# The second layer of an expert block, one half of its rows after the other

## The chip, the core and the metric

The kernel runs on one core of a Trainium2 chip. The metric is the device time of one execution in microseconds (us). The kernel before took 558.54 us, the median of three runs (556.77 to 562.39). The engines are TensorE (PE in the rows; PEld is its weight load), VectorE (DVE), ScalarE (ACT), GpSimd (POOL) and SyncE (SP). Each takes its instructions in the order of its own queue.

## The reference, cut to what matters

A global filter, then a mixture of experts with one expert for each token:

```
X = rfft(x, axis=1);  Y = X * F;  y = irfft(Y)            # x: 8 x 2496 x 256
x = y.reshape(19968, 256)
logits = x @ w_gate + modality_bias[modality_id]          # 8 experts
e_idx = argmax(logits);  gate_w = softmax(logits)[e_idx]
for e in range(8):
    h = relu(x[e_idx == e] @ w1[e])                       # 256 -> 1024
    out[e_idx == e] = gate_w * (h @ w2[e])                # 1024 -> 256
```

## The kernel before, in words

The filter is done as a two-stage Fourier transform by matmuls, for eight groups of 2496 tokens. When a group is done, its tokens are routed, and GpSimd scatters their rows to bins in DRAM by expert (`scatter`, line 786; 20 indirect DMAs for a group). From then on blocks of 256 tokens of one expert are taken from the bins and sent through the two layers, while the next groups are still being transformed. 79 blocks are computed in this draw. The three kinds of work (transform, routing, blocks) lie beside each other until the last group is routed; then only blocks are left.

A block is 256 rows, as two halves of 128 rows (`NI` = 2). The first layer gives `hT`, 1024 hidden columns as eight tiles (`FT` = 8) of 128 partitions by 256 rows. `up(b, q)`, for q from 0 to 3, does two of these tiles: four matmuls (line 945) into a PSUM tile `hps`, and one Relu on ScalarE (line 950) into `hT`. `down(b, q)` is the second layer: in each step it takes the two hidden tiles that belong to q, and for each of them both halves of the rows: four matmuls (line 958) that add to `ops`, a PSUM tile of 128 x 2 x 256 float32, where the first index of the free part is the half. Both halves lie in one 2 KiB bank of PSUM. There are two buffers of `ops`.

`step()` sets the order in which the block's work is written: `up` of the current block, `down` of the block before it, with the same q. So between two steps of `down` there are four matmuls of `up`. At q = 1 the next block is prepared (`turn`): VectorE copies the expert's first weights to `w1` (line 913), later also the second weights to `w2` (line 920), and, in the first 44 blocks, the block's transposed rows to `xT` (line 932).

After the last step of `down`, VectorE multiplies each half of `ops` by the gates of its rows into `osb` (line 970, two instructions), and GpSimd scatters both halves to the output (line 972, two indirect DMAs). `osb` has three buffers; later, every other block takes a buffer of another pool of three, so that a buffer is used again six blocks on. A new tile of `osb` is taken when the gate is written, and its first write waits until both scatters from the old tile in that buffer have landed.

In the first part of the program the order on TensorE, ScalarE and VectorE is as written. In the part with the blocks a scheduler sets the order of instructions on each engine when the program is built, from its own estimates; it also places the waits. Two rules of the code bind it on GpSimd: a scatter to the bins is issued behind the last scatter to the output written before it (`behind("out", 1)`), and it waits for a matmul written shortly before (`paced`).

Of the kernel before, what the change touches and what calls it, by code (L numbers as in the profile page):

```python
# [12 lines left out]
F32 = mybir.dt.float32  # L13
# [5 lines left out]
IOA = bass.IndirectOffsetOnAxis  # L19
ET = mybir.EngineType  # L20

P = 128
# [7 lines left out]
def kernel(  # L30
# [12 lines left out]
    nc = tc.nc  # L43

    B, S, D = x.shape
    NF = S // 2 + 1
    N = B * S
# [5 lines left out]
    FT = F // P  # L53
# [18 lines left out]
    NI = BLK // P  # L72
# [48 lines left out]
    xp = ctx.enter_context(tc.tile_pool(name="fx", bufs=3))  # L121
# [18 lines left out]
    marks = {"ld": [], "up": [], "w1": [], "out": [], "pe": []}  # L140
# [40 lines left out]
    def row_int(expr_ops, base, name):  # L181

        t = fft_pool.tile([P, 1], I, name=name + "_int")
        nc.vector.tensor_copy(t, base)
        for op, v in expr_ops:
            nc.vector.tensor_single_scalar(t, t, v, op=op)
        f = fft_pool.tile([P, 1], F32, name=name)
        nc.vector.tensor_copy(f, t)
        return f
# [26 lines left out]
    NP = NTT // EV  # L216
# [141 lines left out]
    with tc.manual_schedule():  # L358
# [14 lines left out]
        for f_dram, g in ((filt_r, g1), (filt_i, g2)):  # L373
# [5 lines left out]
            out=Lexcl, in_=Lexcl, compare_op=ALU.is_ge, fill=1.0,  # L379
# [8 lines left out]
        half = row_int([(ALU.arith_shift_right, 1)], rows_i, "half")  # L388
# [87 lines left out]
        for s0 in range(0, NS, SPB):  # L476
            for src, dst in ((w2m, a1m), (w2x, a2m)):
                tp = pp.tile([P, EV * D], F32, tag="ps", name="tp")
                for i in range(SPB):
                    nc.tensor.matmul(tp[:KB, i * KB:(i + 1) * KB], lhsT=src[:, s0 + i, :], rhs=perm,  # L480
                                     start=True, stop=True)
# [21 lines left out]
    w2sb = wpool.tile([P, E, FT, D], BF16)  # L503
# [292 lines left out]
    def free_of(ins, group):  # L796
        tc.declare_no_dep(ins.ins, group=group, reason="disjoint rows")
# [136 lines left out]
            nc.vector.tensor_copy(b["meta"], b["xs"][:, :, DW:DW + 2])  # L934

    FQ = 2
    turn_about = [False]

    def up(b, q):
        third = "xs" not in b and len(marks["up"]) % 3 == 2  # L940
        hps = (op if third else hp).tile([P, FQ, NI * P], F32, tag="tr" if third else "hps", name="hps")
        for k in range(FQ):
            ft = q * FQ + k
            for dc in range(DC):
# [4 lines left out]
        marks["pe"].append(mm.ins)  # L949
        nc.scalar.activation(b["hT"][:, q * FQ:(q + 1) * FQ, :], hps, AF.Relu)  # L950

    def down(b, q):
        if q == 0:
            b["ops"] = op.tile([P, NI, D], F32, tag="ops", bufs=2, name="ops")
        for k in range(FQ):
            ft = q * FQ + k
            for i in range(NI):
                nc.tensor.matmul(b["ops"][:, i, :], lhsT=b["hT"][:, ft, i * P:(i + 1) * P],  # L958
                                 rhs=b["w2"][:, ft, :] if b["still"] else w2sb[:, ds(b["e"], 1), ft, :],
                                 start=(ft == 0 and i == 0), stop=(ft == FT - 1 and i == NI - 1))  # L960
        if (q + 1) * FQ == FT:

            turn_about[0] ^= n > begin[B - 1] + NP
            if turn_about[0]:
                osb = xp.tile([P, NI, D], F32, tag="x", name="osb")
            else:
                osb = ep.tile([P, NI, D], F32, tag="osb", bufs=3)
            gate = b["meta"][:, :, 1:2].bitcast(F32)
            for i in range(NI):
                nc.vector.tensor_scalar_mul(osb[:, i, :], b["ops"][:, i, :], gate[:, i, :])  # L970
            for i in range(NI):
                ins = nc.gpsimd.indirect_dma_start(  # L972
                    out=out[:, :], out_offset=IOA(ap=b["meta"][:, i, 0:1], axis=0),
                    in_=osb[:, i, :], in_offset=None, bounds_check=N - 1, oob_is_err=False)
                marks["out"].append(ins.ins)
                free_of(ins, "outs")
                tc.add_to_no_dep_group("outs", ins.ins)

    def pad_bins():

# [11 lines left out]
    class Experts:  # L992
# [36 lines left out]
        def step(self):  # L1029

            if self.q == 0:
                if self.cur is None:
                    self.cur = self.next()
                    self.begin(self.cur)
                self.nxt = None
            if self.cur is None and self.prev is None:
                return False
            if self.cur is not None:
                up(self.cur, self.q)
                if self.q == 1:  # L1040

                    self.nxt = self.next()
            if self.prev is not None:
                down(self.prev, self.q)
            if self.q == 1:
                self.begin(self.nxt)
            self.q += 1
            if self.q == FT // FQ:
                self.prev, self.cur, self.q = self.cur, self.nxt, 0
            return True  # L1050
# [51 lines left out]
    with tc.manual_schedule(engines={ET.PE, ET.Activation, ET.DVE}):  # L1102
# [141 lines left out]
        n = -2 * LONG  # L1244
# [20 lines left out]
    ep = ctx.enter_context(tc.tile_pool(name="expert", bufs=2, side="right", reuse_waits="tile"))  # L1265
# [9 lines left out]
    begin = [(g - TURNED - 2) * GAP for g in range(B)]  # L1275
# [5 lines left out]
    n = max(0, opening[0][1] + WAIT)  # L1281
# [3 lines left out]
    n = 0  # L1285
# [3 lines left out]
    while n <= end or to_bins or opening:  # L1289
# [3 lines left out]
        for g in range(TURNED + 1, B):  # L1293
            k = n - begin[g] - OFF2
# [6 lines left out]
        for g in range(TURNED, B):  # L1301
            k = n - begin[g] - OFF3
# [63 lines left out]
```

## Time and profile before

| | |
|---|---|
| median of three runs | 558.54 us (556.77 to 562.39) |
| the profiled execution | 557.56 us |
| its span, first to last instruction | 555.7 us |
| mean granted TensorE clock | 0.955 of full speed |
| busy share | PE 89%, DVE 68%, ACT 68%, POOL 70% |
| scatters on POOL | 158 to the output, 160 to the bins |

The span is 1.86 us shorter than the device time of the same execution. A row of a timeline gives the start, the duration, the engine, the line, the operation and how many instructions of that kind are merged in it (x4: four); in square brackets stands the idle time before it and who ended it. Matmuls are pipelined, and the duration of one includes its way through the array, so the ends of consecutive matmuls overlap the next starts.

### The profile page before, as it was taken

To read this page: it belongs to the slowest core of one execution; us is meant where nothing else is said; L and a number is where in the kernel's file an instruction comes from. 1 tells how busy PE (TensorE), PEld (TensorE's weight loads), DVE (VectorE), ACT (ScalarE), POOL (GpSimd) and SP (SyncE) were. 2 spreads that over 40 slices of the span, in tenths; PEclk is the share of its full clock that TensorE was granted. 3 is DMA by queue.
4 is the path that set the end of the run, shared out by engine and by line. 5 is a ranking of instruction groups with operands and counts; after the bars stand their busy time and mean duration, and the time that the engine had idled before them with its cause. 6 is when DMAs were issued, how large, how long until landed. Compare 5 with 4: busy or idle time off the path is not lost.

```text
span 555.7 us, 14830 instructions
## 1 busy us (share of the span) xinstructions
PE 493.6 (89%) x4933; PEld 451.8 (81%) x4933; DVE 377.7 (68%) x1139; ACT 376.0 (68%) x692; POOL 390.3 (70%) x427
## 2 busy tenths in 40 slices
PE   3699979687999898999999999998799989999992
PEld 2678868576988798898898988897689989999991
DVE  8866878643678678688879988863465555655541
ACT  4686866775787687788777765565466666666660
POOL 9633378585525776777777777777777777777773
PEclk9978889878999898999999999999899999999996
DMA  9989989779799899989868563253354445565521
GB/s 139 165 127 214 212 173 183 166 176 251 187 198 232 240 201 213 275 215 240 259 178 235 146 185 124 79 173 97 115 120 104 123 121 119 129 135 135 134 96 43
DMA packets 103112, 92.42 MB, mean 166 GB/s; under 512 B 40293, under 2 KB 86725, under 8 KB 102941
## 3 DMA queue, kind: packets, MB, share of 16 engines
q0 software_dynamic: 31936, 50.75, 40.3%
q1 hardware_dynamic: 47795, 29.16, 22.4%
q10 hardware_dynamic: 23302, 11.50, 7.8%
q8 instruction: 43, 0.70, 0.5%
q14 instruction: 36, 0.29, 0.2%
HBM read 60.10 MB, written 46.35 MB: 192 GB/s over the span
## 4 chain that ended last, share of the span: by engine, by line
PE 47%; DMA 25%; DVE 12%; issue 6%; ACT 4%; POOL 4%; DVEq 0%; SPq 0%; POOLq 0%; ACTq 0%
PE hps L945 13%; PE ops L958 13%; DMA out_dram<-osb,metas 11%; DMA bins_d<-yo,pos_i 4%; DMA b_d<-t 3%; DMA b_d<-z 3%; PE ps L545 3%; DMA t<-b_d 2%; PE pz L557 2%; PE lt L691 2%; PE pz L558 2%; PE ps L668 2%; DVE osb L970 2%; DVE xf L580 2%; PE ps L671 1%
## 5 line engine op out<-in xcount | busy, mean ns | idle before, releaser
L950 ACT ACTIVATE hT<-hps 128x512 f16<-128x512 f32 x316 | 187.9, 598 | 93.7 <-PE hps L945 89.2
L972 POOL DMA_INDIRECT out_dram<-osb,metas x158 | 167.7, 1062 | 55.3 <-issue 18.9
L786 POOL DMA_INDIRECT bins_d<-yo,pos_i x160 | 164.8, 1030 | 58.1 <-issue 28.8
L945 PE MATMUL hps<-xT,w 128*128 128x256 f16 x1264 | 200.0, 276 | 6.0 <-DVE xT L932 6.0
L945 PEld LDWEIGHTS <-w 128*128 128x128 f16 x1264 | 148.6, 145 | 10.6 <-DVE xT L932 6.8
L958 PEld LDWEIGHTS <-hT 128*128 128x128 f16 x1264 | 123.1, 98 | 17.9 <-issue 6.8
L958 PE MATMUL ops<-w2sb,hT 128*128 x704 | 113.0, 275 | 1.5 <-issue 1.4
L970 DVE TENSOR_SCALAR osb<-ops,metas 128x256 f32<-128x256 f32 x158 | 69.3, 476 | 46.9 <-DMA out_dram<-osb,metas 35.2
L958 PE MATMUL ops<-w,hT 128*128 128x256 f16 x560 | 83.3, 272 | 2.3 <-DVE osb L970 2.2
L913 DVE COPY w<-w1sb 128x2048 f16 x79 | 56.3, 712 | 41.2 <-PE hps L945 38.2
L572 ACT CAST xf<-ps 104x512 f16<-104x512 f32 x96 | 57.6, 600 | 9.7 <-PE ps L545 8.1
L579 DVE TENSOR_TENSOR p<-xf,g 104x512 f16<-104x512 f16 x96 | 40.2, 419 | 28.4 <-ACT xf L572 28.1
L594 ACT CAST z<-pz 104x512 f16<-104x512 f32 x72 | 42.7, 593 | 13.0 <-PE pz L558 10.7
L545 PE MATMUL ps<-t,w2m 104*104 104x256 f16 x192 | 40.2, 293 | 3.9 <-DMA t<-b_d 2.2
L557 PE MATMUL pz<-p,a1m 104*104 104x256 f16 x144 | 38.9, 287 | 4.8 <-ACT z L594 2.5
L580 DVE TENSOR_TENSOR xf<-xf,g 104x512 f16<-104x512 f16 x96 | 40.4, 420 | 2.8
L248 ACT CAST t<-ps 96x512 f16<-96x512 f32 x52 | 30.3, 582 | 16.2 <-PE ps L244 9.8
L558 PE MATMUL pz<-xf,a2m 104*104 104x256 f16 x144 | 37.8, 286 | 0.6 <-DVE xf L580 0.6
L163 POOL DMA_DIRECT2D xt<-in_x_dram x32 | 23.5, 736 | 19.6 <-PE ps L545 6.7
L668 PE MATMUL ps<-t,wbm 96*128 96x256 f16 x120 | 29.5, 276 | 5.4 <-DMA t<-b_d 3.3
L700 DVE COPY yT<-lt 128x512 f16<-128x512 f16 x60 | 25.1, 418 | 9.1 <-PE lt L696 7.1
L545 PEld LDWEIGHTS <-w2m 104*104 104x104 f16 x192 | 22.6, 138 | 6.7 <-DMA t<-b_d 2.5
(222 smaller groups left out, 753.5 us busy)
## 6 DMA issues: line engine op xcount, KB each, us to landing
xt<-in_x_dram POOLq DMA_DIRECT2D x24, 384.0 KB
t<-b_d SPq DMA_DIRECT2D x22, 384.0 KB
b_d<-z ACTq DMA_DIRECT2D x30, 208.0 KB
xs<-bins_d SPq DMA_DIRECT2D x44, 130.0 KB
b_d<-t ACTq DMA_DIRECT2D x24, 192.0 KB
t<-b_d SPq DMA_DIRECT2D x11, 416.0 KB
w1sb<-in_moe_w_dram POOLq DMA_DIRECT2D x16, 256.0 KB
w2sb<-in_moe_w_dram POOLq DMA_DIRECT2D x8, 512.0 KB
```

What stands on the lines that cost most here:

```text
L545: mm = nc.tensor.matmul(ps[:KB, i, :], lhsT=w2m[:, s + i, :], rhs=st[g]["t2", s // SCH][:, s % SCH + i, :], start=True, stop=True)
L557: nc.tensor.matmul(pz[:KB, i, :], lhsT=a1m[:, s + i, :], rhs=p1[:, i, :], start=True, stop=False)
L558: nc.tensor.matmul(pz[:KB, i, :], lhsT=a2m[:, s + i, :], rhs=p2[:, i, :], start=False, stop=True)
L572: nc.scalar.copy(xf, ps[:KB])
L580: nc.vector.tensor_mul(xf, xf, g2[:, sl, :])
L786: ins = nc.gpsimd.indirect_dma_start(out=bins_d[:, :], out_offset=IOA(ap=st[g]["pos"][:rows, t:t + 1], axis=0), in_=st[g]["yw"][:rows, t, ...
L913: cp = nc.vector.tensor_copy(b["w1"].rearrange("p a f -> p (a f)"), w1sb[:, ds(ej, 1)].rearrange("p o a f -> p (o a f)"))
L945: mm = nc.tensor.matmul(hps[:, k, :], lhsT=b["w1"][:, dc, ft:F:FT], rhs=b["xT"][:, dc].rearrange("p i t -> p (i t)"), start=(dc == 0), sto ...
L950: nc.scalar.activation(b["hT"][:, q * FQ:(q + 1) * FQ, :], hps, AF.Relu)
L958: nc.tensor.matmul(b["ops"][:, i, :], lhsT=b["hT"][:, ft, i * P:(i + 1) * P], rhs=b["w2"][:, ft, :] if b["still"] else w2sb[:, ds(b["e"], ...
L970: nc.vector.tensor_scalar_mul(osb[:, i, :], b["ops"][:, i, :], gate[:, i, :])
L972: ins = nc.gpsimd.indirect_dma_start(out=out[:, :], out_offset=IOA(ap=b["meta"][:, i, 0:1], axis=0), in_=osb[:, i, :], in_offset=None, bou ...
```

## The change

`down(b, q)` now does the four hidden tiles of one half of the rows in a step: q = 0 and 1 are the first 128 rows (hidden tiles 0 to 3, then 4 to 7), q = 2 and 3 the last 128. The number of matmuls and their shapes are the same. After q = 1 the first half is gated and scattered, after q = 3 the second. The tile `osb` is taken at q = 1. Each half now starts its own accumulation (`start` at the hidden tile 0).

```diff
+    HALF = FT // NI
     def down(b, q):
         if q == 0:
             b["ops"] = op.tile([P, NI, D], F32, tag="ops", bufs=2, name="ops")
-        for k in range(FQ):
-            ft = q * FQ + k
-            for i in range(NI):
-                nc.tensor.matmul(b["ops"][:, i, :], lhsT=b["hT"][:, ft, i * P:(i + 1) * P],
-                                 rhs=b["w2"][:, ft, :] if b["still"] else w2sb[:, ds(b["e"], 1), ft, :],
-                                 start=(ft == 0 and i == 0), stop=(ft == FT - 1 and i == NI - 1))
-        if (q + 1) * FQ == FT:
+        i, half = divmod(q, 2)
+        for ft in range(half * HALF, (half + 1) * HALF):
+            nc.tensor.matmul(b["ops"][:, i, :], lhsT=b["hT"][:, ft, i * P:(i + 1) * P],
+                             rhs=b["w2"][:, ft, :] if b["still"] else w2sb[:, ds(b["e"], 1), ft, :],
+                             start=(ft == 0), stop=(ft == FT - 1))
+        if half:
+            if i == 0:
...
+            osb = b["osb"]
             gate = b["meta"][:, :, 1:2].bitcast(F32)
-            for i in range(NI):
-                nc.vector.tensor_scalar_mul(osb[:, i, :], b["ops"][:, i, :], gate[:, i, :])
-            for i in range(NI):
-                ins = nc.gpsimd.indirect_dma_start(
...
+            nc.vector.tensor_scalar_mul(osb[:, i, :], b["ops"][:, i, :], gate[:, i, :])
+            ins = nc.gpsimd.indirect_dma_start(
+                out=out[:, :], out_offset=IOA(ap=b["meta"][:, i, 0:1], axis=0),
+                in_=osb[:, i, :], in_offset=None, bounds_check=N - 1, oob_is_err=False)
```

In the changed kernel the lines are numbered differently: `up` is at 947, `down` at 959, the gate at 972, the scatter to the output at 973.

**TensorE, a block near the end (the 59th).** Here are the rows from the last matmul of its second step to the first of its third, before. In brackets stand the semaphores that an instruction waits for, by the engine that raises them.

```order
L958 MATMUL ops<-w_9060,hT 128x256
L945 LDWEIGHTS w_9116
L945 MATMUL hps<-xT,w_9116 128x256 [waits Activation_49]
L945 LDWEIGHTS w_9116
L945 MATMUL hps<-xT,w_9116 128x256
L945 LDWEIGHTS w_9116
L945 MATMUL hps<-xT,w_9116 128x256
L945 LDWEIGHTS w_9116
L945 MATMUL hps<-xT,w_9116 128x256
L958 LDWEIGHTS hT
L958 MATMUL ops<-w_9060,hT 128x256
```

And with the change, from the second of the six matmuls of `up` that now stand there to the first matmul of the second half:

```order
L947 MATMUL hps<-xT,w_9121 128x256
L947 LDWEIGHTS w_9121
L947 MATMUL hps<-xT,w_9121 128x256
L947 LDWEIGHTS w_9121
L947 MATMUL hps<-xT,w_9121 128x256
L947 LDWEIGHTS w_9121
L947 MATMUL hps<-xT,w_9121 128x256 [waits Activation_49]
L947 LDWEIGHTS w_9121
L947 MATMUL hps<-xT,w_9121 128x256
L959 LDWEIGHTS hT
L959 MATMUL ops<-w_9065,hT 128x256 [waits DVE_49]
```

The scheduler has put six matmuls of `up` in place of four ahead of the third step, and the first matmul of the second half waits for VectorE. Such a wait on VectorE stands at the second half of nearly every block; before, `down` waited for VectorE only at the start of a block, for the gate of the block two before it.

**VectorE, the same block.** Before, from the copy of a `w2` to the one after the gates:

```order
L920 COPY w_9239<-w2sb 128x2048
L913 ISA
L913 COPY w_9237<-w1sb 128x2048 [waits DVE_49,PE_49]
L970 TENSOR_SCALAR osb<-ops,metas 128x256 [waits DMASW5_49,DMAHW4_49,DMASW4_49,PE_49]
L970 TENSOR_SCALAR osb<-ops,metas 128x256
L873 TENSOR_LOAD ej_i
L920 ISA
L920 COPY w_9311<-w2sb 128x2048
```

With the change:

```order
L920 COPY w_9244<-w2sb 128x2048
L972 TENSOR_SCALAR osb<-ops,metas 128x256 [waits DMASW5_49,DMAHW4_49,DMASW4_49,PE_49]
L913 ISA
L913 COPY w_9242<-w1sb 128x2048 [waits DVE_49,PE_49]
L972 TENSOR_SCALAR osb<-ops,metas 128x256 [waits PE_49]
L873 TENSOR_LOAD ej_i
L920 ISA
L920 COPY w_9316<-w2sb 128x2048
```

The gate of the first half has moved ahead of the copy of `w1`; it carries the wait for the two scatters (DMASW) from the buffer's old tile, and the gate of the second half waits for TensorE alone.

**GpSimd, the scatters around the 12th and 13th block, among those of the fourth group's rows to the bins.** Before:

```order
L972 DMA out_0_dram<-osb_4302,metas_2186 19968x256
L786 DMA bins_d<-yo1_107,pos_i_4109 162048x130 x2
L972 DMA out_0_dram<-osb_4302,metas_2186 19968x256
L786 DMA bins_d<-yo1_107,pos_i_4109 162048x130 x3
L972 DMA out_0_dram<-osb_4487,metas_2186 19968x256 x2
```

With the change:

```order
L973 DMA out_0_dram<-osb_4195,metas_2186 19968x256
L786 DMA bins_d<-yo1_107,pos_i_4109 162048x130
L163 DMA xt_4263<-in_x_dram 96x8x256
L973 DMA out_0_dram<-osb_4195,metas_2186 19968x256
L786 DMA bins_d<-yo1_107,pos_i_4109 162048x130 x2
L973 DMA out_0_dram<-osb_4371,metas_2186 19968x256
L786 DMA bins_d<-yo1_107,pos_i_4109 162048x130 x3
L973 DMA out_0_dram<-osb_4371,metas_2186 19968x256
```

The first half of the 13th block's output has moved ahead of three scatters to the bins, and its second half stands where it stood. From the 31st block on, the order of the scatters on GpSimd is the same in both kernels.

## Rows read from the trace of the kernel before

**Rows 1.** The page: span, and busy time of each engine

```profile
span 555.7 us, 14830 instructions
PE 493.6 (89%) x4933; PEld 451.8 (81%) x4933; DVE 377.7 (68%) x1139; ACT 376.0 (68%) x692; POOL 390.3 (70%) x427
```

**Rows 2.** Windows: busy us (x instructions) of each engine, clock, DMA

```profile
core 0: us, PE busy (x) PEld busy (x) DVE busy (x) ACT busy (x) POOL busy (x), PEclk, DMA share, GB/s
120.00:237.00 117.00, 106.53 (x1028) 97.27 (x1028) 79.21 (x259) 86.68 (x167) 73.64 (x77) 0.96 0.94 225
...
480.00:545.00 65.00, 64.51 (x590) 60.64 (x587) 37.64 (x75) 43.01 (x72) 50.30 (x47) 1.00 0.50 124
```

**Rows 3.** Groups on POOL, 236.8 to 543.1: busy, mean ns, idle before

```profile
L972 POOL DMA_INDIRECT out_dram<-osb,metas x130 | 138.9, 1068 | 38.9 <-issue 16.5 <-DMA out_dram<-osb,metas 7.9 <-DVE osb L970 4.9
L786 POOL DMA_INDIRECT bins_d<-yo,pos_i x93 | 95.5, 1027 | 29.6 <-issue 11.9 <-DMA out_dram<-osb,metas 3.4 <-PE lt L696 2.8
```

**Rows 4.** Timeline of POOL around its last long idle time

```profile
232.94 1.11 POOL L972 DMA_INDIRECT out_dram<-osb,metas  x1 [0.30 <-issue]
234.35 0.97 POOL L786 DMA_INDIRECT bins_d<-yo,pos_i  x1 [0.30 <-issue]
236.87 0.97 POOL L786 DMA_INDIRECT bins_d<-yo,pos_i  x1 [1.55 <-PE lt L696]
238.14 0.97 POOL L786 DMA_INDIRECT bins_d<-yo,pos_i  x1 [0.30 <-issue]
```

**Rows 5.** Waits, 340 to 545: us in total, times, longest

```profile
DVE osb L970 <- DMA out_dram<-osb,metas: 35.2, 16, 5.0
PE ops L958 <- DVE osb L970: 2.2, 3, 1.4
```

**Rows 6.** The chain that ended last, its piece at 475 to 480

```profile
475.33 4.12 DMA out_dram<-osb,metas
...
479.67 0.48 DVE osb L970
```

**Rows 7.** Timeline of PE, 474 to 481

```profile
473.88 0.60 PE L958 MATMUL ops<-w,hT 128*128 128x256 f16 x4
474.32 0.60 PE L945 MATMUL hps<-xT,w 128*128 128x256 f16 x4
474.75 0.60 PE L958 MATMUL ops<-w,hT 128*128 128x256 f16 x4
...
475.63 0.60 PE L958 MATMUL ops<-w,hT 128*128 128x256 f16 x4
...
479.56 0.60 PE L945 MATMUL hps<-xT,w 128*128 128x256 f16 x4
480.60 0.60 PE L958 MATMUL ops<-w,hT 128*128 128x256 f16 x4 [0.44 <-DVE osb L970]
```

**Rows 8.** Timeline of DVE, the gate at 479.67

```profile
479.67 0.88 DVE L970 TENSOR_SCALAR osb<-ops,metas 128x256 f32<-128x256 f32 x2 [3.14 <-DMA out_dram<-osb,metas]
```

**Rows 9.** Groups on DVE, 479.6 to 546: the gates

```profile
L970 DVE TENSOR_SCALAR osb<-ops,metas 128x256 f32<-128x256 f32 x42 | 18.3, 477 | 9.1 <-PE ops L958 5.9 <-DMA out_dram<-osb,metas 3.1
```

**Rows 10.** Groups on DVE, 120 to 237: the gates

```profile
L970 DVE TENSOR_SCALAR osb<-ops,metas 128x256 f32<-128x256 f32 x24 | 10.7, 476 | 0.1
```

**Rows 11.** Timeline, 536 to 548: the last blocks

```profile
536.05 0.60 PE L945 MATMUL hps<-xT,w 128*128 128x256 f16 x4
539.11 0.60 PE L958 MATMUL ops<-w,hT 128*128 128x256 f16 x4
539.54 0.60 PE L945 MATMUL hps<-xT,w 128*128 128x256 f16 x4
539.74 0.88 DVE L970 TENSOR_SCALAR osb<-ops,metas 128x256 f32<-128x256 f32 x2 [2.45 <-PE ops L958]
542.05 0.98 POOL L972 DMA_INDIRECT out_dram<-osb,metas  x1 [0.30 <-issue]
542.60 2.35 PE L958 MATMUL ops<-w,hT 128*128 128x256 f16 x20
543.24 0.88 DVE L970 TENSOR_SCALAR osb<-ops,metas 128x256 f32<-128x256 f32 x2 [2.62 <-PE ops L958]
544.00 0.98 POOL L972 DMA_INDIRECT out_dram<-osb,metas  x1 [0.96 <-DVE osb L970]
544.98 0.88 DVE L970 TENSOR_SCALAR osb<-ops,metas 128x256 f32<-128x256 f32 x2 [0.87 <-PE ops L958]
547.85 0.98 POOL L972 DMA_INDIRECT out_dram<-osb,metas  x1 [0.30 <-issue]
```

More of the change, by code (lines that the diff above doesn't have):

```diff
@@ L936 @@
     FQ = 2
+    HALF = FT // NI
+    assert FT // FQ == 2 * NI
     turn_about = [False]
@@ L954, in down @@
             b["ops"] = op.tile([P, NI, D], F32, tag="ops", bufs=2, name="ops")
-        for k in range(FQ):
-            ft = q * FQ + k
-            for i in range(NI):
-                nc.tensor.matmul(b["ops"][:, i, :], lhsT=b["hT"][:, ft, i * P:(i + 1) * P],
-                                 rhs=b["w2"][:, ft, :] if b["still"] else w2sb[:, ds(b["e"], 1), ft, :],
-                                 start=(ft == 0 and i == 0), stop=(ft == FT - 1 and i == NI - 1))
-        if (q + 1) * FQ == FT:
[L963 to L967, printed above, removed]
-            gate = b["meta"][:, :, 1:2].bitcast(F32)
-            for i in range(NI):
-                nc.vector.tensor_scalar_mul(osb[:, i, :], b["ops"][:, i, :], gate[:, i, :])
-            for i in range(NI):
-                ins = nc.gpsimd.indirect_dma_start(
[L973 to L977, printed above, removed]
@@ new lines, in down @@
+        i, half = divmod(q, 2)
[5 more added lines that the diff above has]
+            if i == 0:
+                turn_about[0] ^= n > begin[B - 1] + NP
+                if turn_about[0]:
+                    b["osb"] = xp.tile([P, NI, D], F32, tag="x", name="osb")
+                else:
+                    b["osb"] = ep.tile([P, NI, D], F32, tag="osb", bufs=3, name="osb")
+            osb = b["osb"]
+            gate = b["meta"][:, :, 1:2].bitcast(F32)
+            nc.vector.tensor_scalar_mul(osb[:, i, :], b["ops"][:, i, :], gate[:, i, :])
+            ins = nc.gpsimd.indirect_dma_start(
+                out=out[:, :], out_offset=IOA(ap=b["meta"][:, i, 0:1], axis=0),
+                in_=osb[:, i, :], in_offset=None, bounds_check=N - 1, oob_is_err=False)
+            marks["out"].append(ins.ins)
+            free_of(ins, "outs")
+            tc.add_to_no_dep_group("outs", ins.ins)
```

## The prediction

> **What bounds the kernel now.** I read the page first. TensorE is busy 89% of the span, GpSimd 70% [rows 1]; from this alone TensorE would be the bound. The windows by stage say more: from 480 on TensorE is busy 64.5 of 65 us at the full clock, while between 120 and 237 GpSimd has only 73.6 busy us of 117 [rows 2]. Then I read the groups of GpSimd from 236.8 to 543.1. There 130 scatters to the output and 93 to the bins take 138.9 + 95.5 us, and the short idle time before each adds 38.9 + 29.6: together 302.9 of 306.3 us [rows 3]. A busy share hides this, because 0.3 us of each slot counts as idle; the slots follow each other without a hole. GpSimd is saturated from its last long idle time, which ends at 236.87 [rows 4], until 543.03, and a slot is about 1.3 us (236.87 to 238.14).
>
> So scatters run late behind the gates, and buffers of `osb` come free late. VectorE's gate waited for the landing of such a scatter 16 times, 35.2 us in all, but TensorE waited for a gate only three times, 2.2 us [rows 5]. The reader is to see why in one instance. A scatter issued at 475.33 lands after 4.12 us; the gate that needs its buffer starts at 479.67 [rows 6]. The block of that gate had its last matmuls issued from 475.63; TensorE ran on with the next block and the one after until it stopped for 0.44 us, and began the next `ops` at 480.60 [rows 7]. TensorE may thus run on by a whole block (3.49 us, 536.05 to 539.54 [rows 11]) behind a gate that is late. After 480.60 TensorE has no such stop, and at the end both engines arrive almost together: GpSimd's last backlog is gone at 543.03, where it waits 0.96 us for a gate [rows 11].
>
> **The change, part by part.** Matmuls, gates, scatters and copies are the same in number and shape, so no engine's work changes. Moved are the gate and the scatter of the first half. Added is one wait, which the built order shows: the first matmul of a second half waits for VectorE, because both halves of `ops` lie in one bank and the gate of the first half reads it.
>
> First what this wait costs where the gate is on time. VectorE starts 0.03 us after the last matmul ends (539.11 + 0.60 to 539.74 [rows 11]), one gate takes 0.476 us [rows 10], and TensorE starts 0.05 us after (479.67 + 0.88 to 480.60 [rows 7, 8]): 0.56 us. In the rows the third step starts 0.27 us after the end of the second (473.88 + 0.60 = 474.48 to 474.75 [rows 7]) with four matmuls of `up` between. The scheduler has put six there; at 0.109 us each (0.435 / 4, 474.32 to 474.75) two more make the cover 0.49 us. A wait of 0.07 us is left for a block. Between nothing (a gate a little quicker) and 0.37 us (VectorE is found in a copy and is 0.3 us late) I take 0.07, since in the rows VectorE is free at that point.
>
> Then where the gate is late. Now the first half's gate carries the wait for the buffer, and TensorE needs this gate half a block later, not a block and a half: it stops in the middle of the same block. The landing itself does not move, as GpSimd has no hole and its order from the 31st block on is unchanged. So the second half of the block whose gate starts at 479.67 [rows 8] starts at 479.67 + 0.476 + 0.05 = 480.20; in the rows that was 474.75 [rows 7]. This is the main term. The stops ahead of it lie under the same landings and are not added.
>
> From there the sum runs on TensorE. 42 gates start from 479.67 on, 21 blocks [rows 9]; from the second half of the first to that of the last but one are 19 blocks of 3.49 + 0.07 us, 67.6 us: 547.8. Then ten matmuls to the end of that block's (1.09), eight of the last block's first half (0.87), its gate with no `up` to cover it (the matmul's 0.27 to its end plus 0.56, less the 0.11 of its own slot: 0.72), eight more and the end of the last (0.87 + 0.16): 551.5. The last gate and the start of its scatter add 0.03 + 0.48 + 0.28 (543.24 + 0.48 to 544.00 [rows 11]): 552.3. Before, it started at 547.85, which is 2.90 us after the last matmul's end (542.60 + 2.35 = 544.95), since four scatters stood in a row behind two late pairs of gates; now it is 0.8 us, which is already in the sum. The end moves by 552.3 − 547.85 = +4.45 us.
>
> Two smaller terms are set against each other. In the last long idle time of GpSimd (1.55 us [rows 4]) the order now has a first half's scatter ahead of the bins' scatter that it waited for: one slot, −1.3 us for all that follows. Against it, in the transform's stage up to 237 there are 24 gates, 12 blocks [rows 10], and any wait of TensorE for a first gate there delays the matmul that GpSimd's bins wait for. Below, the cost is nothing, as transform matmuls lie between most halves; above, with VectorE 68% busy (79.2 of 117 us [rows 2]) and no cover at all, (0.56 + 0.2) x 12 = 9.1 us. I take 1.3 us, near the lower end, since the order has cover at almost every block. What such waits cost after 237 is hidden behind GpSimd's backlog until that is gone.
>
> The profiled execution took 557.56 us for a span of 555.7: 557.56 + 4.45 = **562.0 us**. It was 0.98 us under the median of 558.54, so the forecast is 0.6% over the median. About 1% is what a measurement of this kernel can tell from no change.
>
> The Trainium skill, PSUM — Partial Sum Buffer, section "PSUM bank collisions raise a hardware error", speaks against this change: two engines must not touch one bank at once even in different columns, the chip does not arbitrate, and accesses are to be guarded by bank. By this the wait has to stand, and the sum is 562.0; could the halves be kept apart by address alone, it would be the 556.9 of the first rival. No run here shows it yet.
>
> **The rivals.** *The wait is hidden and GpSimd still sets the end.* If TensorE, with gates half a block earlier, keeps ahead of GpSimd, the slots just run on past 543.03 without the 0.96 us wait: the last scatter starts at 542.05 + 4 x 1.28 = 547.17 in place of 547.85, 556.9 us, and 555.6 with the slot at 235. For it: the two engines are balanced at the end. Against it: the 35.2 us of late gates [rows 5], which now reach TensorE at once.
>
> *Slower, by the transform's stage.* VectorE's queue is in order, and a first gate behind a multiplication that waits for ScalarE holds TensorE. With 0.6 us for each of the 12 blocks, 7.2 in place of 1.3: 567.9 us. It decides against no change once TensorE's waits there pass 1.3 + 2.1 = 3.4 us (562.0 + 2.1 is 1% over the median). For it: VectorE's load there; against it: the cover.
>
> *Faster, by GpSimd's early holes.* Before 237 GpSimd was idle for a third of the time [rows 2]. If first halves bring three scatters into it, 3 x 1.3 + 0.7 = 4.6 us: 553.0. Against it: the holes are there because nothing was ready, and the end is TensorE's. That the change doesn't do what it says is excluded by the order.
>
> **How the numbers follow.** Forecast 0.48 (its own range 559 to 565, with 0 to 0.2 us of wait for a block and one slot more or less), hidden 0.22, slower 0.22, faster 0.08. Of the forecast's 0.48 some 0.08 lies over 564.1. So faster by over 1% (under 553.0) 0.07, slower by over 1% 0.30, within 1% 0.63. The range of 554 to 569 leaves out most of the faster case and the upper end of the waits (0.37 us for each of 19 blocks, 567.7, plus some of the 9.1).
>
> **What would show it.** Right: TensorE's row "`ops` waits for `osb`" grows from 2.2 to some 10 us or more, with stops of some us in the middle of blocks between 370 and 480; after it blocks come every 3.56 us, not 3.49; GpSimd has holes in the last 30 us; the last scatter starts 0.8 us after the last matmul. Wrong: GpSimd without a hole up to the end (first rival); TensorE's waits on VectorE before 237 over 3 us (second); GpSimd saturated from well before 236 (third); or copies of weights behind a late gate that stop `up`, which I cost at nothing, since a weight copy is needed a block after it.

## The result, and the profile after

The changed kernel takes 562.58 us (median of 18 runs, 558.95 to 567.64), the kernel before 559.16 beside it (18 runs): a ratio of **1.007**, 95% interval 1.0043 to 1.0098, some 3.9 us. The ratios here and below leave out executions in a slower state that some runs show, and they are not the quotients of the medians beside them (here the medians lie 3.4 us apart). The forecast was 562.0, within 1% and so no change by its own measure. With 18 runs on each side the interval is narrower than that: the kernel has become slower by 0.4 to 1.0%. The profiled execution took 563.28 us, its span is 561.5.

The page, answering to [rows 1], and the windows from 480 on, answering to [rows 2]:

```profile
span 561.5 us, 14803 instructions
PE 500.1 (89%) x4933; PEld 451.8 (80%) x4933; DVE 382.7 (68%) x1139; ACT 375.3 (67%) x692; POOL 389.9 (69%) x427
```

```profile
480.00:545.00 65.00, 65.00 (x587) 60.43 (x586) 41.75 (x73) 43.34 (x74) 49.31 (x45) 1.00 0.48 125
545.00:562.00 17.00, 7.50 (x66) 6.44 (x64) 2.90 (x6) 3.98 (x7) 6.42 (x7) 0.86 0.13 43
```

No engine has more work. Before, TensorE's last matmul ended at 544.95 [rows 11]; now 7.5 us of matmuls lie behind 545. The waits from 340 to 545 (total, times, longest) show who was late, against [rows 5]:

```profile
DVE osb L972 <- DMA out_dram<-osb,metas: 11.9, 5, 3.8
PE ops L959 <- DVE osb L972: 8.2, 5, 2.7
```

VectorE waits less for landings (35.2 us before), since TensorE now stands with it (2.2 us before). But 2.2 us is not all that late gates cost TensorE before. Here is a row of the same list and an instance, before, in the timelines of VectorE and TensorE:

```profile
PE hps L945 <- DVE xT L932: 5.7, 4, 3.0
```

```profile
391.51 0.88 DVE L970 TENSOR_SCALAR osb<-ops,metas 128x256 f32<-128x256 f32 x2 [5.04 <-DMA out_dram<-osb,metas]
392.30 0.41 DVE L932 COPY xT<-pT 128x512 f16<-128x512 f16 x1
392.77 0.66 PE L945 MATMUL hps<-xT,w 128*128 128x256 f16 x4 [2.97 <-DVE xT L932]
```

The copy of `xT` stands behind the late gate in VectorE's queue, and the next `up` needs it. At 380.21, 385.85 and 392.77 this stopped TensorE for 4.9 us, and a fourth such copy for 0.8 (414.08). So TensorE stood 7.9 us before and 8.2 now: the stops have moved from `up` to the second half of a block, and they have hardly grown.

One instance of the change, the counterpart of [rows 6 to 8], in the timelines of TensorE and of VectorE:

```profile
468.27 0.82 PE L947 MATMUL hps<-xT,w 128*128 128x256 f16 x6
471.03 0.60 PE L959 MATMUL ops<-w,hT 128*128 128x256 f16 x4 [1.94 <-DVE osb L972]
...
477.44 0.82 PE L947 MATMUL hps<-xT,w 128*128 128x256 f16 x6
478.18 0.60 PE L959 MATMUL ops<-w,hT 128*128 128x256 f16 x4
...
481.01 0.82 PE L947 MATMUL hps<-xT,w 128*128 128x256 f16 x6
481.75 0.60 PE L959 MATMUL ops<-w,hT 128*128 128x256 f16 x4
```

```profile
470.49 0.48 DVE L972 TENSOR_SCALAR osb<-ops,metas 128x256 f32<-128x256 f32 x1 [2.31 <-DMA out_dram<-osb,metas]
```

The gate of a first half waits 2.31 us for the landing of an old scatter; TensorE has six matmuls of `up` as cover and then stops in the middle of that block. After it the second halves come every 3.57 us (478.18, 481.75). The end, answering to [rows 11], in the timeline of all engines:

```profile
551.40 0.97 POOL L973 DMA_INDIRECT out_dram<-osb,metas  x1 [0.86 <-DVE osb L972]
551.51 0.48 DVE L972 TENSOR_SCALAR osb<-ops,metas 128x256 f32<-128x256 f32 x1 [0.39 <-PE ops L959]
552.04 1.03 PE L959 MATMUL ops<-w,hT 128*128 128x256 f16 x8 [0.57 <-DVE osb L972]
552.67 0.97 POOL L973 DMA_INDIRECT out_dram<-osb,metas  x1 [0.30 <-issue]
553.12 0.48 DVE L972 TENSOR_SCALAR osb<-ops,metas 128x256 f32<-128x256 f32 x1 [1.12 <-PE ops L959]
553.95 0.97 POOL L973 DMA_INDIRECT out_dram<-osb,metas  x1 [0.31 <-DVE osb L972]
```

GpSimd waits for gates here (0.86 us in the first of these rows), from 537.3 on in seven holes of over 0.4 us: TensorE sets the end. Before, three scatters were still to start when TensorE was done (544.95; the last at 547.85).

### The profile page after: what moved, and what is told of

It reads as the page before. It is cut to its first block, busy times and chain, and to the rows that moved or that the text cites. A ratio compares the mean times of both kernels' runs of the same rounds, so it can differ in the third digit from the quotient of the medians.

```text
span 561.5 us, 14803 instructions
## 1 busy us (share of the span) xinstructions
PE 500.1 (89%) x4933; PEld 451.8 (80%) x4933; DVE 382.7 (68%) x1139; ACT 375.3 (67%) x692; POOL 389.9 (69%) x427
## 5 line engine op out<-in xcount | busy, mean ns | idle before, releaser
L973 POOL DMA_INDIRECT out_dram<-osb,metas x158 | 169.9, 1076 | 58.4 <-DVE osb L972 24.9
L786 POOL DMA_INDIRECT bins_d<-yo,pos_i x160 | 162.7, 1017 | 58.2 <-issue 23.5
L972 DVE TENSOR_SCALAR osb<-ops,metas 128x256 f32<-128x256 f32 x158 | 75.6, 479 | 48.6 <-PE ops L959 36.1
```

The lines of the kernel that those rows point to most:

```text
L786: ins = nc.gpsimd.indirect_dma_start(out=bins_d[:, :], out_offset=IOA(ap=st[g]["pos"][:rows, t:t + 1], axis=0), in_=st[g]["yw"][:rows, t, ...
L973: ins = nc.gpsimd.indirect_dma_start(out=out[:, :], out_offset=IOA(ap=b["meta"][:, i, 0:1], axis=0), in_=osb[:, i, :], in_offset=None, bou ...
```

## The experiments

My theory: the change costs because a late gate stops TensorE in its own block, and that brings TensorE's end behind GpSimd's. The rivals: the order of the matmuls costs by itself; the short wait at each block's second half costs by itself; GpSimd's slots are what moved.

In the first four runs the kernel before took 681.3 us (23 runs), with pauses of all engines (the last section shows one), so these ratios tell of that condition, not of the one above.

**The order alone.** Halves one after the other, but both gated and scattered after the last step.

```diff
-        if half:
-            if i == 0:
+        if q == 3:
...
+            for i in range(NI):
+                nc.vector.tensor_scalar_mul(osb[:, i, :], b["ops"][:, i, :], gate[:, i, :])
```

> The matmuls of the second layer run over one half of the rows and then the other, but both halves are gated and scattered after the second one, as before. Theory (a second half waits for the gate of the first, because both lie in one bank): no such wait exists here, so the time is that of before, 558.5 to 560 us, a ratio of 0.999 to 1.002, and TensorE's waits for a gate stay at 2 to 3 us. Rival 1 (the order of the matmuls itself costs: the whole of the hidden tiles is wanted earlier and four matmuls in a row add to the same place): 562 to 563 us, ratio 1.005 to 1.009. Rival 2 (the early gates and scatters disturb the transform's stage): as before, since no gate moves.

Measured: 682.84 us, ratio 1.0025 (0.9984 to 1.0066). The order alone costs nothing that can be told there. But 3.9 us would be 0.6% of that time and lie within this interval, and the run was not made at 558 us: the first rival is not excluded.

**A bank for each half.** The tile is taken at the start of each half, so that the two halves lie in two buffers, one bank each.

```diff
-        if q == 0:
-            b["ops"] = op.tile([P, NI, D], F32, tag="ops", bufs=2, name="ops")
         i, half = divmod(q, 2)
+        if half == 0:
+            b["ops"] = op.tile([P, NI, D], F32, tag="ops", bufs=2, name="ops")
```

> The change, but each half takes a PSUM buffer of its own (the two buffers of ops now hold the two halves, so a block has no second buffer behind it). Theory: TensorE no longer waits in the middle of a block; behind a late gate it may run on half a block (1.75 us) and the 0.07 us of each block go: 558 to 559.5 us, ratio 0.997 to 1.001, TensorE's waits for a gate under 4 us in place of 8.9. Rival 1 (order of the matmuls): 562 to 563. Rival 2 (early gates disturb the transform's stage): 561.5 to 563, since gates and scatters are as early as in the change.

Measured: 665.23 us, ratio 0.9738 (0.9678 to 0.9798), a gain of 2.6% in that condition; on it hangs nothing for the 0.7%.

**A deeper ring of `osb`.** A buffer of the other pool now holds the tiles of two blocks, so that one is used again nine blocks on instead of six.

```diff
-                turn_about[0] ^= n > begin[B - 1] + NP
+                if n > begin[B - 1] + NP:
+                    turn_about[0] = (turn_about[0] + 1) % 3
+                if turn_about[0] == 1:
+                    both_osb[0] = xp.tile([P, 2, NI, D], F32, tag="x", name="osb")
                 if turn_about[0]:
-                    b["osb"] = xp.tile([P, NI, D], F32, tag="x", name="osb")
+                    b["osb"] = both_osb[0][:, turn_about[0] - 1]
```

> The change, with the osb tiles used again nine blocks on in place of six (a buffer of the second pool holds two blocks' tiles). Theory: the gates are no longer late, TensorE's stops between 370 and 480 us (8.2 us in six stops) go, the 0.08 us a block stay; GpSimd without a hole then sets the end, last scatter some 4 us earlier: 557.5 to 559.5 us, ratio 0.996 to 1.001. Rival 3 (the wait of 0.08 to 0.4 us in every block of the last stage is what costs, 36 blocks, 3 to 5 us): 562 us, ratio 1.005, since every block still has it. Rivals 1 and 2: 562 as well.

Measured: 675.41 us, ratio 0.9886 (0.9824 to 0.9948).

**Halves in the last 35 blocks only.**

```diff
+    def down(b, q):
+        (down_halves if b["still"] else down_whole)(b, q)
```

> The change only for the last 35 blocks (from about 420 us on); the 44 blocks before are done as before. Theory: the landings that TensorE meets after 450 us are GpSimd's and do not move, so nearly the whole cost is there: 561 to 562.5 us, ratio 1.003 to 1.007, with stops in the middle of blocks between 450 and 480 us. Rival 2 (the cost comes from the transform's stage): the time of before, 558.5 to 559.5.

Measured: 680.82 us, ratio 0.997 (0.9928 to 1.0011): no cost to be seen there. Whether the cost of 0.7% lies in these blocks this run can't say, as the change itself was not timed in that condition and this kernel was not timed at 558 us.

The next runs were beside a kernel before of 558.26 us (29 runs).

**A bank for each half, again** (the same edit).

> The two-bank kernel again, since in the first runs the kernel before itself took 681 us in place of 559 and all engines stood still together at times; here it is wanted where the kernel before takes about 559. Theory (a second half waits for the first half's gate in the same bank): 558 to 559.5 us, ratio 0.997 to 1.001, TensorE's waits for a gate under 4 us. Rivals 1 and 2 (order of the matmuls; early gates): ratio 1.004 or more.

Measured: 563.1 us, ratio **1.0052** (1.0018 to 1.0087). My theory had this wrong. TensorE's waits for a gate were to be under 4 us; from 340 on they are 5.2, and 6.8 more for copies of `xT` behind late gates. The last matmul ends at 552.28, nearly as late as in the change (553.07), though no second half waits for the first one's gate. And TensorE isn't what ends here. The last matmuls and scatters, in the timeline:

```profile
549.93 2.35 PE L959 MATMUL ops<-w,hT 128*128 128x256 f16 x20
550.32 0.97 POOL L973 DMA_INDIRECT out_dram<-osb,metas  x1 [0.30 <-issue]
...
552.87 0.97 POOL L973 DMA_INDIRECT out_dram<-osb,metas  x1 [0.30 <-DVE osb L972]
554.15 0.97 POOL L973 DMA_INDIRECT out_dram<-osb,metas  x1 [0.30 <-issue]
```

GpSimd has no idle time but its 0.3 us to the last scatter, 554.15; it is the bound, as in the kernel before, and its scatters have become longer. The groups of scatters to the output from 400 on (busy, mean ns of one), first of the kernel before, then of this one:

```profile
L972 POOL DMA_INDIRECT out_dram<-osb,metas x93 | 99.0, 1065 | 29.0 <-issue 14.6 <-DMA out_dram<-osb,metas 7.0 <-DVE osb L970 5.5
```

```profile
L973 POOL DMA_INDIRECT out_dram<-osb,metas x94 | 104.9, 1116 | 28.7 <-issue 14.6 <-DMA out_dram<-osb,metas 5.8 <-DVE osb L972 5.8
```

94 scatters at 51 ns more are 4.8 us. The last scatter comes 6.3 us later than before, of which 2.1 were there at the 209th of all scatters (399.18, 397.12 before): the longer scatters account for about all of the rest. One of the long ones, in the timeline of this kernel:

```profile
501.23 0.69 DVE L913 COPY w<-w1sb 128x2048 f16 x1 [0.82 <-PE hps L947]
501.35 1.70 POOL L973 DMA_INDIRECT out_dram<-osb,metas  x1 [0.30 <-DMA out_dram<-osb,metas]
...
502.23 0.68 DVE L920 COPY w<-w2sb 128x2048 f16 x1
...
503.34 0.97 POOL L973 DMA_INDIRECT out_dram<-osb,metas  x1 [0.30 <-issue]
```

The scatter that began 0.12 us behind a copy of `w1` and met the copy of `w2` took 1.70 us; the next, with no copy beside it, 0.97. Before, two gates (0.88 us) stood between the two copies, now one does (0.48). In the kernel before 21 scatters from 400 on overlap two copies as well, and none of them takes over 1.36 us; here it is 19, up to 1.77. That gave a new theory for this kernel: GpSimd's slots.

**The change with the deeper ring, again** (the edit of the ring).

> The change with osb tiles used again nine blocks on, once more where the kernel before takes about 559. Theory: no late gates, so TensorE's stops of 1 to 3 us between 370 and 480 go, and GpSimd without a hole sets the end: 557.5 to 559.5 us, ratio 0.996 to 1.001. Rival 3 (the short wait in every block of the last stage costs): ratio 1.005.

Measured: 558.65 us, ratio **0.9991** (0.9954 to 1.0028). The cost in time is gone, as expected. The stops are not all gone: three of 0.8 to 1.2 us are left between 449 and 474. Its waits from 340 on:

```profile
DVE osb L976 <- DMA out_dram<-osb,metas: 4.4, 3, 1.7
PE ops L960 <- DVE osb L976: 3.7, 4, 1.2
```

and its end, in the timeline:

```profile
543.64 1.03 PE L960 MATMUL ops<-w,hT 128*128 128x256 f16 x8 [0.58 <-DVE osb L976]
...
548.57 0.97 POOL L977 DMA_INDIRECT out_dram<-osb,metas  x1 [0.30 <-issue]
549.85 0.97 POOL L977 DMA_INDIRECT out_dram<-osb,metas  x1 [0.30 <-issue]
```

TensorE is done at 544.67, 8.4 us earlier than in the change, and GpSimd ends without a hole. The wait at each block's second half still stands there (0.19 us between the starts of two matmuls instead of 0.11), so that wait is not what costs as long as GpSimd sets the end.

**The kernel before with the deeper ring** (the same edit).

> The kernel before with osb tiles used again nine blocks on, the change not made. Theory: before, late gates cost almost nothing, because TensorE could run on a block and a half and GpSimd set the end anyway: ratio 0.996 to 1.001, TensorE's waits for a gate from 2.2 to about 0 us. Rival 4 (a deeper ring is worth 4 us to any kernel, and has nothing to do with the shared bank): ratio 0.992 to 0.994.

Measured: 558.06 us, ratio **0.9985** (0.995 to 1.002). TensorE is done 6.6 us earlier than in the kernel before (its last gates start at 538.39, against 544.98 in [rows 11]), and the last scatter stays:

```profile
538.39 0.88 DVE L974 TENSOR_SCALAR osb<-ops,metas 128x256 f32<-128x256 f32 x2 [0.87 <-PE ops L959]
...
548.31 0.98 POOL L976 DMA_INDIRECT out_dram<-osb,metas  x1 [0.30 <-DMA out_dram<-osb,metas]
```

So the kernel before is bound by GpSimd at its end, and late gates cost it nothing. TensorE's waits for a gate did not go to 0: they are 2.4 us (2.2 without the ring); what went are the 5.7 us behind copies of `xT`.

These two runs say less of the change than they seem to. The ring takes 6.6 us off TensorE's end in the kernel before and 8.4 in the change. With the ring in both, TensorE still ends 6.3 us later in the change (544.67 and 538.35; 8.1 without it). So the ring hides most of what the change costs TensorE behind GpSimd's end; it does not show that late gates are that cost.

**A bank for each half and the deeper ring.** By mistake this run had the ring of the change: it repeats the run with two banks.

> Placeholder for a look at the two-bank kernel a second time on the same chip: as its other run within 0.5%.

Measured, in a single run: 564.84 us, the two banks' time within 0.5%. It says nothing of the ring.

The last four ran beside a kernel before of 559.49 us (29 runs).

**A bank for each half and the deeper ring**, now with both edits.

> A bank of its own for each half, as in the earlier run that gave 1.0052, and with it the ring of osb that is used again only nine blocks on. Theory (GpSimd's slots): with two banks GpSimd has no hole up to the last scatter, and its scatters from 400 on are longer than before (1.115 us against 1.07) because more of them run beside a copy of weights on VectorE; a deeper ring doesn't touch that, so the ratio stays at 1.002 to 1.008, GpSimd still without a hole at the end, scatters from 400 on at 1.09 us or more. Rival (late gates are what costs there too): the ratio falls to 0.997 to 1.001, as it did for the change with the deeper ring.

Measured: 560.75 us, ratio 1.003 (0.9988 to 1.0072): the interval holds both theories. The trace speaks for the slots: TensorE's last matmul ends at 542.85, GpSimd goes on without a hole to 551.64, and its scatters from 400 on take 1.116 us, as with two banks alone.

**No copy of the second weights.** In the last 35 blocks TensorE reads them where they lie, as in the first 44; made in three kernels.

```diff
-            b["still"] = n > end and "xs" not in b
+            b["still"] = False
```

With two banks:

> A bank for each half, and in the last 35 blocks no copy of the second weights: TensorE reads them where they lie, as it does in the first 44 blocks. Theory (scatters are stretched by copies on VectorE): mean scatter from 400 on falls from 1.115 to 1.04 us or less, none of 1.7 us is left, the slot falls by 0.07 us, some 110 slots give 7 us back on GpSimd, of which TensorE (it has to find its matmuls in time, and reads the weights by a register) leaves about half: ratio 0.988 to 0.999. Rival (the length of a scatter has nothing to do with the copies): scatters stay at 1.10 us, ratio 1.002 to 1.010.

Measured: 557.53 us, ratio **0.9952** (0.9911 to 0.9993), the lowest ratio of the runs at 558 us and the only one there whose interval lies below the kernel before, by a hair. Against the two banks alone it is 1.0% less (0.9952 / 1.0052, each beside its own kernel before). The scatters fell as a group, though less than the 1.04 expected; none takes over 1.5 us:

```profile
L973 POOL DMA_INDIRECT out_dram<-osb,metas x94 | 100.6, 1070 | 29.3 <-issue 14.9 <-DVE osb L972 5.9 <-DMA out_dram<-osb,metas 5.8
```

In the kernel before:

> The kernel before without the copy of the second weights in the last 35 blocks. Theory (stretched scatters): scatters from 400 on fall from 1.07 to 1.03 us or less, gates wait for landings less than 35 us, GpSimd's end comes 4 us earlier, TensorE then sets the end: ratio 0.988 to 0.997. Rival (copies are beside the path): 0.998 to 1.003; if reading the weights by a register costs TensorE time in each block, above 1.003.

Measured: 557.2 us, ratio 0.9971 (0.9934 to 1.0009), at the edge of what was expected and not to be told from no change; but the scatters did not fall (1.068 us), the gates waited for landings as long as before (35.9 us from 340 on), and the last scatter came at 550.33, not 4 us earlier. In this kernel nothing speaks for my theory. The scatters that start up to 0.35 us behind the start of a copy are as many as before (14) and take longer, 1.34 us against 1.25: fewer copies alone do not make shorter scatters.

In the change:

> The change without the copy of the second weights in the last 35 blocks. Theory (late gates stop TensorE, and they are late because GpSimd runs behind): with shorter scatters fewer gates are late; of the change's 0.7% against the kernel before half or more goes: within 0.3% of the kernel before without these copies if TensorE has no stop of over 1 us left after 400, else above it by the sum of the stops. Rival (the wait at each block's second half costs by itself): 0.5% or more above the kernel before without these copies, with no stop of over 1 us.

Measured: 565.51 us, ratio **1.0153** (1.0096 to 1.0211), 1.8% above the kernel before without these copies, with no stop of over 1 us after 400. My theory fell here. The rival's numbers came, but the wait is the smaller part of it, as these rows show. Two blocks in the timelines of TensorE and of GpSimd:

```profile
513.83 0.82 PE L947 MATMUL hps<-xT,w 128*128 128x256 f16 x6
514.57 0.68 PE L959 MATMUL ops<-w2sb,hT 128*128 x4
515.08 0.38 PE L947 MATMUL hps<-xT,w 128*128 128x256 f16 x2
...
517.48 0.82 PE L947 MATMUL hps<-xT,w 128*128 128x256 f16 x6
518.22 0.79 PE L959 MATMUL ops<-w2sb,hT 128*128 x4
518.85 0.38 PE L947 MATMUL hps<-xT,w 128*128 128x256 f16 x2
```

```profile
513.24 0.97 POOL L973 DMA_INDIRECT out_dram<-osb,metas  x1 [1.18 <-DVE osb L972]
...
516.95 0.97 POOL L973 DMA_INDIRECT out_dram<-osb,metas  x1 [1.18 <-DVE osb L972]
```

GpSimd has a hole in every block from 503 on: with scatters of 1.002 us it has caught up, and TensorE is the bound. Its blocks come every 3.71 us (the 60th to the 78th) against 3.49 with two banks and no copy. Of the 0.22 us some 0.08 is the wait (six matmuls of `up` take 0.74 to the next start, 513.83 to 514.57, in place of 0.66). Most of the rest lies behind it: the four matmuls of `down` take 0.51 and 0.63 us here, 0.54 on average over these blocks, not 0.44. They read the weights by a register; without a wait ahead of them, in the same kernel with two banks, they show no such loss. The profiled execution is the fastest of the six (562.23 us). From the 34th block to the last matmul it takes TensorE 5.3 us more than the kernel before without these copies; what the other executions add to make 1.8% no trace shows.

The change itself reads by a register in its first 44 blocks. There, too, more than the 0.08 us of the wait is lost: from the 38th to the 42nd block it takes 3.86 us a block, the kernel before 3.73.

Together, from the profiled executions:

| | ratio | last matmul ends | last scatter starts | scatter to the output, from 400 on |
|---|---|---|---|---|
| before | 1 | 544.95 | 547.85 | 1.065 |
| change | 1.007 | 553.07 | 553.95 | 1.090 |
| change, ring | 0.9991 | 544.67 | 549.85 | 1.098 |
| before, ring | 0.9985 | 538.35 | 548.31 | 1.069 |
| two banks | 1.0052 | 552.28 | 554.15 | 1.116 |
| two banks, ring | 1.003 | 542.85 | 551.64 | 1.116 |
| two banks, no `w2` copy | 0.9952 | 547.61 | 549.12 | 1.070 |
| before, no `w2` copy | 0.9971 | 547.43 | 550.33 | 1.068 |
| change, no `w2` copy | 1.0153 | 551.98 | 552.78 | 1.002 |

Times in us. TensorE sets the end where the last matmul and the last scatter are 0.8 to 0.9 us apart, which only the two kernels with both halves in one bank and the old ring show. In the others they are 1.5 us or more apart, and GpSimd still has scatters left. Three of them (before, before without the `w2` copy, two banks without it) have one or two holes of over 0.4 us on GpSimd in the last 8 us up to the last scatter: there both engines arrive almost together.

## Why the prediction was right, point by point

- **What bounds.** Right: both engines arrive almost together, and of the two GpSimd binds. The kernel before is GpSimd's (the deeper ring takes 6.6 us from TensorE and nothing from the time). The change had some 2 us to hide in (547.85 − 0.88 − 544.95, with the 0.88 us from the last matmul's end to the last scatter that the change shows), and needed more.
- **The wait where the gate is on time**, 0.07 us a block: 0.08 in 15 of the 19 blocks from the 60th to the 78th (none where the scheduler has ten matmuls of `up` there), a period of 3.556, 3.56 forecast. That is 1.2 us for the forecast's 1.3. Its size is not safe elsewhere: with the weights read by a register a block lost 0.22 us.
- **The late gate stops its own block**, the main term: the stops are there, their price is not shown. TensorE stops at second halves at 381.53, 387.06, 393.69, 454.80 and 471.03, 0.5 to 2.7 us, 8.2 us in all ("some 10 or more" was said). But the prediction read the kernel before's stops as 2.2 us and overlooked the 5.7 behind copies of `xT` (it named such copies, of weights, among the signs of being wrong, and priced them at nothing). Against 7.9 us before, the change adds little here. The first matmul of `ops` comes 5.35 us later in the 34th block (377.93, 372.58 before), ahead of every such stop, 6.25 later in the 61st and 7.39 in the 79th, and the last matmul ends 8.13 later. This is no sum of causes, since a TensorE that comes earlier waits longer for the same landing; it does say that most of the delay was there before the first late gate.
- **Where luck helped.** The 59th block's second half starts at 481.75, 1.55 us later than forecast. The forecast let one landing set it, and had it that landings do not move; in fact the block's own gate was on time (481.21) and the stop came three blocks earlier, at 471.03. The landing that ended it, of the 50th block's second scatter, came 3.17 us later than before (470.30, 467.13): the scatter started 1.83 us later (466.27, 464.44), and it took 4.03 us in place of 2.69. With the landing where it was, TensorE would not have stopped there.
- **From there to the end**: 71.3 us forecast from the second half to the last matmul's end, 553.07 − 481.75 = 71.32 measured; the last scatter 0.88 us later, 0.8 forecast. Hidden and faster, the first and third rival, fall by the holes in GpSimd's last 17 us and by the time; the first became true only with the deeper ring.
- **The two small terms.** The slot won, −1.3 us, didn't come. The scatter did move ahead (235.95), and the one to the bins that it passed came later still. GpSimd's last long idle time, the answer to [rows 4]:

```profile
235.95 0.99 POOL L973 DMA_INDIRECT out_dram<-osb,metas  x1 [0.30 <-DVE osb L972]
239.53 0.96 POOL L786 DMA_INDIRECT bins_d<-yo,pos_i  x1 [2.60 <-ACT t L248]
```

  The long idle time ends 2.66 us later than at 236.87. Of this 1.41 was there before the first block could do anything (the first matmul of `ops` at 124.61, 123.20 before); over all profiled executions of these last runs that start lies between 119.8 and 124.8. Counting scatters, the 121st starts at 278.0 to 280.4 in the three kernels with whole blocks and at 275.8 to 281.6 in the seven with halves. Counted from the first matmul of `ops` it comes 154.6 to 156.3 us later with whole blocks and 156.0 to 159.1 with halves, 2.6 us more on average. TensorE shows it more clearly: from its first matmul of `ops` to the first of the 34th block it takes 249.3 to 249.8 us in the three kernels with whole blocks and 252.5 to 254.9 in the seven with halves, those with two banks included. So the two terms did not cancel: in these ten traces halves cost TensorE 2.8 to 5.7 us over the first 33 blocks, and GpSimd some 2.6 up to the 121st scatter. It is not by the way that the second rival gave, TensorE's wait for a first gate: in the change those waits come to 0.9 us over the first 33 blocks. Whether the order of the matmuls or the early gates and scatters do it stays open; neither the order alone nor halves in some of the blocks was run at 558 us.
- **The sum.** +4.45 us was forecast; the profiled executions differ by 5.72, the medians by 3.4, and the ratio says 3.9. The difference of the profiled ends, 6.1, is the 4.45, the 1.55 of the 59th block and 0.1. That the sum comes so near is in part luck: a landing that moved and a first stage that cost more than nothing took the place of the landing that was forecast. What is shown is the path at the end: TensorE's end moved behind GpSimd's.
- **What I had wrong** is a price in the text that the result didn't need: that halves kept apart would give the first rival's 556.9. They gave 1.0052. The price took GpSimd's slot as a constant 1.28 us [rows 11]; from 400 on a slot is 1.38 already in the kernel before, and 1.42 with two banks (1.116 and 0.31 between). I put the difference down to the gate that has moved between the two weight copies; no run moves that gate by itself. By the rule of the Trainium skill in PSUM — Partial Sum Buffer, section "PSUM bank collisions raise a hardware error", the wait has to stand with one bank; with two it could be left out, and the trace agrees that it was (0.11 us between the starts at every second half from the 60th block on). No run shows a collision.

## What to carry to other kernels

Splitting a result into halves moves a wait for a late buffer forward as well. With one shared bank it stopped TensorE in the same block, at the second half; with two banks the copies behind the gate and the next matmuls of `ops` stopped instead (6.8 and 5.2 us), and TensorE ended as late. When counting what a late instruction stops, follow everything behind it in its queue, not only the row that names it. Where two engines end within 1% of each other, price a change against both ends, and look at what its moved instructions run beside: a saturated engine's slot is no constant. A deeper ring of the buffer that is late, in both kernels, tells whether late buffers set the time; if it speeds up an engine in both, it can also hide another cost of that engine, so compare the engines' ends too.

## What the runs showed of the hardware

**Scatters beside copies.** In the nine traces at 558 us, from 400 on, a scatter to the output with no weight copy beside it takes 0.97 to 1.00 us (355 of them, mean 0.98); one that starts up to 0.35 us behind the start of a single copy beside it 1.31 on average (95); with two copies beside it up to 1.77 (99, mean 1.30). The copies grow as well, from 0.69 us: here, in the change's timeline, a scatter beside a copy that started first, and a copy beside a scatter that started first:

```profile
501.40 0.68 DVE L920 COPY w<-w2sb 128x2048 f16 x1
501.54 1.39 POOL L973 DMA_INDIRECT out_dram<-osb,metas  x1 [0.31 <-DVE osb L972]
...
504.57 0.98 POOL L973 DMA_INDIRECT out_dram<-osb,metas  x1 [0.30 <-issue]
...
505.09 0.98 DVE L920 COPY w<-w2sb 128x2048 f16 x1
```

The Trainium skill, SBUF — State Buffer, section "SBUF: two separate sides", has a reason: VectorE, in its quick modes, and GpSimd lock one pair of ports, and whoever comes second waits for the whole instruction. These rows agree. The 107 scatters that start 0.05 to 0.5 us behind the start of the one copy beside them end 0.84 to 0.87 us behind that copy's end (501.54 + 1.39 is 0.85 behind 501.40 + 0.68), however much of the copy was left (0.20 to 0.65 us). The extra time is 0.13 us less than what was left, so about the first 0.13 us of a scatter's 0.98 go on beside the copy.

**A wait ahead of matmuls that read by a register.** The four matmuls behind it took 0.51 to 0.63 us (mean 0.54) instead of 0.44 in the 60th to the 78th block of the change without the `w2` copy, seen above. Why, no run here isolates.

**All engines at once.** In the condition of the first four runs, the timeline of the order-only kernel:

```profile
445.89 0.14 PEld L947 LDWEIGHTS <-w 128*128 128x128 f16 x1
447.34 0.16 DVE L751 TENSOR_TENSOR off<-off,psO 128x8 f32<-128x8 f32 x1 [3.15 <-remote]
447.37 1.08 ACT L952 ACTIVATE hT<-hps 128x512 f16<-128x512 f32 x2 [2.97 <-remote]
...
448.02 0.60 PE L947 MATMUL hps<-xT,w 128*128 128x256 f16 x4 [1.86 <-ACT hT L952]
```

From 446.0 to 447.3 nothing starts on TensorE, VectorE and ScalarE. From 20 us on, that trace has 23 stretches of over 1 us of this kind, 35 us in all; the kernel before at 558 us has four, 8 us. This is far from all of the 122 us that the kernel before takes longer there, and what the rest is no run shows. Two banks and the deeper ring, with the change, took 2.6 and 1.1% off the time in that condition; why is not shown either.
